# Float64 weights unpacked into adjacent words, from paged DRAM

## The chip, the cores and the metric

The kernel runs on one core of a Trainium2 chip. The metric is the device time of one execution in microseconds; the median of three runs is given beside the profiled execution.

## The reference, cut to what matters

Three stages, each on 2304 tokens of width 512 (4 batches of 576 tokens, 8 heads of 64):

```
attention   softmax(q k^T / 8 within a causal window of 64) v, per head, float32
dense       xn = x / sqrt(mean(x^2) + 1e-6) * rms_g
            g = xn @ w_gate;  val = xn @ w_val;  out = (g * sigmoid(g) * val) @ w_out     d_ff = 1536
top-2       8 experts 512 -> 1024 -> 512, two per token by noisy logits, weighted sum
```

`w_gate`, `w_val` (512 x 1536) and `w_out` (1536 x 512) are float64; everything else is float32. [...]

## The kernel before, in words

The dense stage is cut into 6 blocks of 384 tokens (j) and 12 chunks of 128 hidden units (fc); a step s = 12 j + fc does one chunk for one block. A step is two halves of products (`m1_half`, gate and value, 12 matmuls of 128 x 384 each, because activations and weights are each split into a high and a low part), tanh and products on the vector engines, and the output products (`m1_out`). Attention for the next block is laid between the steps.

The float64 weights are converted once, while block 0 runs, and stay in SBUF as float32: `gv[fc]` holds 512 columns of gate and 512 of value, `wo[fc]` 512 columns of the output weights, two chunks to a page. For every chunk there are three float64 tiles (c = 0, 1, 2), each 128 partitions x 512 numbers, that is 1024 32-bit words.

- `load_w` (lines 334 to 344) brings a tile into a raw page by one DMA on SP's queue. For gate and value, a partition gets four runs of 128 numbers (1 KB each); for `w_out`, one run of 4 KB.
- `conv_a` (346 to 350) is two ScalarE instructions: the high words, read as float32 and scaled, written back in place, every second word (line 349); the low words, read as unsigned integers and scaled into place as integers, also in place (350).
- `conv_b` (352 to 365) clamps the high words in place (line 361; on VectorE, or from chunk 2 on GpSimd for c = 0 and 2), shifts them left by 3 and ors in the low words (363, VectorE, written over the low words), and takes the sign from the high words into the float32 destination (364, VectorE).
- `split_w` and `split_o` (369 to 386) make the high and low parts of a chunk for each step: a ScalarE copy (372, 383) and a subtraction on VectorE or GpSimd (375, 384).

All of this draws on one pool of 24 pages of 4 KB per partition (tag "pg", line 68): the raw tiles, gv (12), wo (6), and the split parts of a step (three pages a step). A page is free again when the last instruction on its tile is done.

The written order is a table of slots, three to a step: chunk fc is loaded two slots before its first `conv_a`, `conv_a(fc, c)` stands in slot i + c and `conv_b(fc, c)` in slot i + c + 1 (lines 802 to 808), where i is the first slot of step fc - 2. A planner in the compiler takes this order as priorities and decides, from its own costs, where each instruction goes in its engine's queue; each engine then works its queue in order.

Of the kernel before, what the change touches and what calls it, by code (L numbers as in the profile page):

```python
# [7 lines left out]
F32 = mybir.dt.float32  # L8
F32R = mybir.dt.float32r
BF = mybir.dt.bfloat16  # L10
I32 = mybir.dt.int32
U32 = mybir.dt.uint32
AF = mybir.ActivationFunctionType
ALU = mybir.AluOpType
# [5 lines left out]
F64_HI = 122879.9921875 * 2.0 ** -112  # L20
# [3 lines left out]
def tile_window_attention_swiglu_top2(  # L24
# [16 lines left out]
    nc = tc.nc  # L41
    P = 128
# [1 line left out]
    N, E = noise.shape  # L44
    DM = H * D
    KD = DM // P
    FF = w_gate.shape[1]
    NF = FF // P
    F2 = w1.shape[2]
    NF2 = F2 // P  # L50
    HP = H // 2
# [18 lines left out]
    def page(dt, name):  # L70
        return pages.tile([P, 1024], dt, name=name, tag="pg", bufs=NPG)
# [30 lines left out]
    for h in range(2):  # L102
        s = slice(h * 64, h * 64 + 64)
        lo = float(-64 * h)
# [32 lines left out]
    CLP = (0, 2)  # L137
# [192 lines left out]
    gv, wo = {}, {}  # L330

    RAW = {}

    def load_w(fc, cs=(0, 1, 2)):
        fs = slice(fc * P, fc * P + P)
        srcs = (w_gate[:, fs].rearrange("(k p) f -> p k f", p=P), w_val[:, fs].rearrange("(k p) f -> p k f", p=P),
                w_out[fs, :])
        for c in cs:
            t = page(I32, f"raw{fc}_{c}")
            if c < 2:  # L340
                nc.sync.dma_start(t.rearrange("p (k f) -> p k f", k=KD), srcs[c].bitcast(I32))
            else:
                nc.sync.dma_start(t, srcs[c].bitcast(I32))
            RAW[fc, c] = t.rearrange("p (n w) -> p n w", w=2)

    def conv_a(fc, c):
        raw = RAW[fc, c]
        hi, lo = raw[:, :, 1].bitcast(F32), raw[:, :, 0]
        nc.scalar.activation(hi, hi, AF.Copy, scale=2.0 ** -112)
        nc.scalar.activation(lo, lo.bitcast(U32), AF.Copy, scale=0.936 * 2.0 ** -29)  # L350

    def conv_b(fc, c):
        raw = RAW.pop((fc, c))
        if c == 0:
            gv[fc] = page(F32, f"gv{fc}")
        if c == 2 and fc % 2 == 0:
            t = page(F32, f"wo{fc}")
            wo[fc], wo[fc + 1] = t[:, :512], t[:, 512:]
        dst = wo[fc] if c == 2 else gv[fc][:, c * 512:c * 512 + 512]
        hi, lo = raw[:, :, 1], raw[:, :, 0]  # L360
        (nc.gpsimd if c in CLP and fc > 1 else nc.vector).tensor_scalar(
            hi.bitcast(F32), hi.bitcast(F32), F64_HI, -F64_HI, op0=ALU.min, op1=ALU.max)
        nc.vector.scalar_tensor_tensor(lo, hi, 3, lo, op0=ALU.logical_shift_left, op1=ALU.bitwise_or)
        nc.vector.scalar_tensor_tensor(dst.bitcast(I32), hi, -0x80000000, lo, op0=ALU.bitwise_and,
                                       op1=ALU.bitwise_or)

    WS = {}

    def split_w(s):
        fc = s % NF  # L370
        h, l = page(F32R, f"gvH{s}"), page(F32R, f"gvL{s}")
        nc.scalar.activation(h, gv[fc], AF.Copy)  # L372
        for c, eng in enumerate((nc.vector, nc.gpsimd if s in GH else nc.vector) if s < NF else (nc.vector,)):
            f = slice(512 * c, 512 * c + 512) if s < NF else slice(0, 1024)
            eng.tensor_tensor(l[:, f], gv[fc][:, f], h[:, f].bitcast(F32), op=ALU.subtract)  # L375
        WS[s] = [h, l]
        if s > 0:
            split_o(s)

    def split_o(s):  # L380
        fc = s % NF
        o = page(F32R, f"woHL{s}")
        nc.scalar.activation(o[:, :512], wo[fc], AF.Copy)  # L383
        nc.gpsimd.tensor_tensor(o[:, 512:], wo[fc], o[:, :512].bitcast(F32),  # L384
                                                           op=ALU.subtract)
        WS[s].append(o)
# [3 lines left out]
    def m1_half(s, part):  # L390
        j = s // NF
        h, l = WS[s][:2]
        ps = bank(f"gv{s}_{part}", [P, TB])
        n = 0
        for kk in range(KD):
            c = slice(part * 512 + kk * P, part * 512 + kk * P + P)
            for a, b in ((h[:, c], xnH[j][:, kk, :]), (h[:, c], xnL[j][:, kk, :]), (l[:, c], xnH[j][:, kk, :])):
                nc.tensor.matmul(ps, a, b, start=n == 0, stop=n == 3 * KD - 1)  # L398
                n += 1
        PG[s, part] = ps  # L400
# [21 lines left out]
    def m1_out(s):  # L422
        j, fc = divmod(s, NF)
        hh = HT.pop(s)
        o = WS.pop(s)[2]
        if fc == 0:
            X2[j] = [psum.tile([P, 512], F32, name=f"x2_{j}_{t}", tag=f"x2_{t}", bufs=1) for t in range(TT)]
        for t in range(TT):
            c = slice(t * P, t * P + P)
            for n, (a, b) in enumerate(((hh[:, 0, c], o[:, :512]), (hh[:, 0, c], o[:, 512:]), (hh[:, 1, c], o[:, :512]))):  # L430
                nc.tensor.matmul(X2[j][t], a, b, start=fc == 0 and n == 0, stop=fc == NF - 1 and n == 2)  # L431
# [350 lines left out]
    for c in range(3):  # L782
        at(WL[c], load_w, 0, (c,))
    at(WL[3], load_w, 1)
    at(CS[0], conv_a, 0, 0)
    at(CS[1], conv_b, 0, 0)
    at(CS[2], conv_a, 0, 1)
    at(CS[3], conv_b, 0, 1)
    at(CS[4], split_w, 0)
    at(13, norm_a, 0)  # L790
    at(14, norm_b, 0)
    at(15, norm_c, 0)
    at(16, after_norm, conv_a, 0, 2)
    at(16, after_norm, conv_b, 0, 2)
    at(16, after_norm, split_o, 0)
    for c in range(3):
        at(17, after_norm, conv_a, 1, c)
        at(17, after_norm, conv_b, 1, c)
    at(WL[4], load_w, 2)
    for i in range(18):  # L800
        run(i)
# [36 lines left out]
    for s in range(NB * NF):  # L838
        j, fc = divmod(s, NF)
# [101 lines left out]
    for c in sorted(set(CAPS)):  # L941
        for e in range(E):
            if CAPS[e] == c and (e == 0 or CAPS[e - 1] != c):
                n = next((i for i in range(e, E) if CAPS[i] != c), E)
# [203 lines left out]
```

## Time and profile before

| | us |
|---|---|
| median of 3 runs (lowest, highest) | 1116.79 (1116.41, 1118.46) |
| profiled execution | 1118.05 |
| its span, first to last instruction | 1116.3 |
| PE busy | 1055.7 (95%) |
| VectorE (DVE) busy | 614.8 (55%) |
| ScalarE (ACT) busy | 555.1 (50%) |
| GpSimd (POOL) busy | 439.9 (39%) |
| DMA packets | 116408, of which 82048 under 512 B and 94576 under 2 KB |

The busy shares are averages over stages with different limits. In a row, PE is the matrix engine and PEld its weight loads, DVE is VectorE, ACT ScalarE, POOL GpSimd, and SPq the queue of SyncE, which issues DMAs; a number such as L364 is the line of the kernel. The arrow in a name such as gv<-raw goes from the tile read to the tile written.

### The profile page before, as it was taken

What the parts mean: (1) busy time and instruction counts of PE and PEld (TensorE: products, weight loads), DVE (VectorE), ACT (ScalarE), POOL (GpSimd) and SP (SyncE); (2) the same over time, 40 slices, a digit from 0 to 9 for tenths busy, and PEclk for the clock granted to TensorE, in tenths of its full rate; (3) what the DMA queues carried; (4) which work ended last, traced back from release to release, by engine and by line L of the source; (5) the groups of instructions that cost most, each with busy time, mean ns of one, the idle gap of its engine ahead of it and who ended that gap; (6) DMA issues with size and microseconds to landing.
All of it is one profiled execution on the core that took longest, in us unless ns stands there. A gap on an engine that the chain in (4) does not pass through costs nothing. (4 is left out here: it accounts for less than half of the span.)

```text
span 1116.3 us, 17685 instructions
## 1 busy us (share of the span) xinstructions
PE 1055.7 (95%) x6452; PEld 940.9 (84%) x6452; DVE 614.8 (55%) x1620; ACT 555.1 (50%) x1265; POOL 439.9 (39%) x456
## 2 busy tenths in 40 slices
PE   7688889999999999999999999899999999999993
PEld 6577778989899998989989888798989898989882
DVE  4899995666565575656666743342425253434330
ACT  6767766656555665655552513333334343433420
POOL 4366662352154225214422336333434354444311
PEclk9799999999999999999999999899999999999997
DMA  7846527111120211100021407435445444455312
GB/s 176 243 138 206 147 67 256 35 44 43 30 55 12 70 32 43 44 15 2 1 67 24 147 12 191 108 108 100 142 96 147 95 140 95 140 99 152 79 15 27
DMA packets 116408, 101.64 MB, mean 91 GB/s; under 512 B 82048, under 2 KB 94576, under 8 KB 116320
## 3 DMA queue, kind: packets, MB, share of 16 engines
q0 software_dynamic: 17904, 49.07, 18.5%
q1 hardware_dynamic: 98416, 51.42, 16.5%
q8 instruction: 52, 0.85, 0.3%
q14 instruction: 36, 0.29, 0.1%
HBM read 80.55 MB, written 19.92 MB: 90 GB/s over the span
## 5 line engine op out<-in xcount | busy, mean ns | idle before, releaser
L398 PE MATMUL gv<-xnH,gvH 128*128 128x384 f32 x576 | 204.2, 356 | 4.1 <-ACT xnH L325 3.2
L889 PE MATMUL y<-wH,hh 128*128 128x512 f32 (+1 forms) x608 | 203.4, 401 | 0.0
L398 PE MATMUL gv<-xnH,gvL 128*128 128x384 f32 x576 | 196.3, 343 | 4.5 <-DVE gvL L375 4.5
L398 PE MATMUL gv<-xnL,gvH 128*128 128x384 f32 x576 | 196.2, 341 | 0.0
L431 PE MATMUL x<-woHL,hh 128*128 128x512 f32 x648 | 174.1, 403 | 4.9 <-ACT hh L416 4.1
L384 POOL TENSOR_TENSOR woHL<-wo,woHL 128x512 fp32r<-128x512 f32 x72 | 99.3, 1380 | 146.5 <-ACT woHL L383 146.3
L431 PEld LDWEIGHTS x<-woHL,hh 128*128 128x128 f32 x648 | 118.8, 189 | 27.9 <-ACT hh L416 4.9
L889 PEld LDWEIGHTS y<-wH,hh 128*128 128x128 f32 (+1 forms) x608 | 113.8, 187 | 29.6 <-issue 0.2
L910 POOL DMA_INDIRECT out_dram<-ys,tid x38 | 62.2, 1636 | 190.7 <-ACT ys L903 145.2
L600 DVE TENSOR_TENSOR wL<-st,wH 128x1024 fp32r<-128x1024 f32 x64 | 78.3, 1226 | 100.9 <-ACT wH L599 98.3
L713 PE MATMUL h<-xph,wL 128*128 128x272 f32 (+3 forms) x448 | 133.3, 298 | 0.1
L713 PE MATMUL h<-xpl,wH 128*128 128x272 f32 (+3 forms) x448 | 133.4, 298 | 0.0
L713 PE MATMUL h<-xph,wH 128*128 128x272 f32 (+3 forms) x448 | 133.3, 298 | 0.0
L723 DVE SCALAR_TENSOR_TENSOR hh<-h,hh 128x272 fp32r<-128x272 f32 (+6 forms) x232 | 69.8, 325 | 111.1 <-ACT hh L719 91.8
L889 PE MATMUL y<-wL,hh 128*128 128x512 f32 (+2 forms) x328 | 129.1, 397 | 0.0
L719 ACT ACTIVATE hh<-h 128x160 fp32r<-128x160 f32 (+4 forms) x184 | 61.5, 343 | 128.6 <-PE h L713 86.8
L398 PEld LDWEIGHTS gv<-xnH,gvH 128*128 128x128 f32 x576 | 109.6, 191 | 7.7 <-ACT xnH L325 4.0
L398 PEld LDWEIGHTS gv<-xnH,gvL 128*128 128x128 f32 x576 | 109.2, 190 | 6.3 <-DVE gvL L375 5.9
L398 PEld LDWEIGHTS gv<-xnL,gvH 128*128 128x128 f32 x576 | 109.6, 190 | 0.8
L375 DVE TENSOR_TENSOR gvL<-gv,gvH 128x1024 fp32r<-128x1024 f32 (+1 forms) x73 | 90.8, 1245 | 15.0 <-ACT gvH L372 12.3
L245 POOL TENSOR_TENSOR pm<-pm,st 128x384 f32<-128x384 f32 x48 | 41.1, 857 | 134.5 <-DVE st L244 101.0
L372 ACT ACTIVATE gvH<-gv 128x1024 fp32r<-128x1024 f32 x72 | 75.6, 1050 | 22.7 <-PE gv L398 15.2
(208 smaller groups left out, 1925.9 us busy)
## 6 DMA issues: line engine op xcount, KB each, us to landing
vw<-in_v_dram SPq DMA_DIRECT2D x60, 128.0 KB
raw<-in_moe_w_gate_dram SPq DMA_DIRECT2D x12, 512.0 KB
raw<-in_moe_w_val_dram SPq DMA_DIRECT2D x12, 512.0 KB
raw<-in_moe_w_out_dram SPq DMA_DIRECT2D x12, 512.0 KB
out_dram<-zero SPq DMA_DIRECT2D x1, 4864.0 KB
qs<-in_q_dram SPq DMA_DIRECT2D x48, 96.0 KB
ks<-in_k_dram SPq DMA_DIRECT2D x48, 96.0 KB
x2d<-xs SPq DMA_DIRECT2D x18, 256.0 KB
```

The lines of the kernel that those rows point to most:

```text
L245: nc.gpsimd.tensor_tensor(p, p, st[:, :, 3:4].to_broadcast([P, 3, P]), op=ALU.mult)
L372: nc.scalar.activation(h, gv[fc], AF.Copy)
L375: eng.tensor_tensor(l[:, f], gv[fc][:, f], h[:, f].bitcast(F32), op=ALU.subtract)
L384: nc.gpsimd.tensor_tensor(o[:, 512:], wo[fc], o[:, :512].bitcast(F32), op=ALU.subtract)
L398: nc.tensor.matmul(ps, a, b, start=n == 0, stop=n == 3 * KD - 1)
L431: nc.tensor.matmul(X2[j][t], a, b, start=fc == 0 and n == 0, stop=fc == NF - 1 and n == 2)
L600: nc.vector.tensor_tensor(lo, a, ho.bitcast(F32), op=ALU.subtract)
L713: nc.tensor.matmul(ps, w, x, start=i == 0, stop=i == 3 * KD - 1)
L719: nc.scalar.activation(hh[:, c0 - p0:c1 - p0], ps[:, c0 - lo:c1 - lo], AF.Relu)
L723: nc.vector.scalar_tensor_tensor(hh[:, l.start + a - s.start:l.start + b - s.start], ps[:, a + p0 - lo:b + p0 - lo], 0.0, hh[:, a:b].bitca ...
L889: nc.tensor.matmul(ps[:a.shape[1]], a, b, start=i == 0, stop=i == len(terms) - 1)
L910: nc.gpsimd.indirect_dma_start(out=out, out_offset=bass.IndirectOffsetOnAxis(ap=r[:m], axis=0), in_=y[:m], in_offset=None, compute_op=ALU. ...
```

## The change

The three float64 weights lie in DRAM as pages of 128 x 512 numbers, one for each chunk, so that every load is 4 KB of adjacent bytes per partition. ScalarE writes the high words to their float32 destination (`target`: half of a gv page, or half of a wo page) as adjacent words, and the low words as adjacent words into the first half of the raw page. VectorE or GpSimd clamps in the destination; the shift writes the low words in the raw page; the sign step writes the destination in place. The destination's page is taken in `conv_a` instead of `conv_b`. The number of instructions on each engine stays the same.

```diff
--- before.py
+++ after.py
@@ -44,8 +44,7 @@
     N, E = noise.shape
     DM = H * D
     KD = DM // P
-    FF = w_gate.shape[1]
-    NF = FF // P
+    NF = w_gate.shape[0]
     F2 = w1.shape[2]
     NF2 = F2 // P
     HP = H // 2
@@ -332,37 +331,35 @@
     RAW = {}
 
     def load_w(fc, cs=(0, 1, 2)):
-        fs = slice(fc * P, fc * P + P)
-        srcs = (w_gate[:, fs].rearrange("(k p) f -> p k f", p=P), w_val[:, fs].rearrange("(k p) f -> p k f", p=P),
-                w_out[fs, :])
         for c in cs:
             t = page(I32, f"raw{fc}_{c}")
-            if c < 2:
-                nc.sync.dma_start(t.rearrange("p (k f) -> p k f", k=KD), srcs[c].bitcast(I32))
-            else:
-                nc.sync.dma_start(t, srcs[c].bitcast(I32))
-            RAW[fc, c] = t.rearrange("p (n w) -> p n w", w=2)
+            nc.sync.dma_start(t, (w_gate, w_val, w_out)[c][fc].bitcast(I32))
+            RAW[fc, c] = t
+
+    def target(fc, c):
+        if c < 2:
+            if fc not in gv:
+                gv[fc] = page(F32, f"gv{fc}")
+            return gv[fc][:, c * 512:c * 512 + 512]
+        if fc not in wo:
+            t = page(F32, f"wo{fc}")
+            wo[fc], wo[fc ^ 1] = t[:, :512], t[:, 512:]
+        return wo[fc]
+
 
     def conv_a(fc, c):
         raw = RAW[fc, c]
-        hi, lo = raw[:, :, 1].bitcast(F32), raw[:, :, 0]
-        nc.scalar.activation(hi, hi, AF.Copy, scale=2.0 ** -112)
-        nc.scalar.activation(lo, lo.bitcast(U32), AF.Copy, scale=0.936 * 2.0 ** -29)
+        words = raw.rearrange("p (n w) -> p n w", w=2)
+        nc.scalar.activation(target(fc, c), words[:, :, 1].bitcast(F32), AF.Copy, scale=2.0 ** -112)
+        nc.scalar.activation(raw[:, :512], words[:, :, 0].bitcast(U32), AF.Copy, scale=0.936 * 2.0 ** -29)
 
     def conv_b(fc, c):
-        raw = RAW.pop((fc, c))
-        if c == 0:
-            gv[fc] = page(F32, f"gv{fc}")
-        if c == 2 and fc % 2 == 0:
-            t = page(F32, f"wo{fc}")
-            wo[fc], wo[fc + 1] = t[:, :512], t[:, 512:]
-        dst = wo[fc] if c == 2 else gv[fc][:, c * 512:c * 512 + 512]
-        hi, lo = raw[:, :, 1], raw[:, :, 0]
-        (nc.gpsimd if c in CLP and fc > 1 else nc.vector).tensor_scalar(
-            hi.bitcast(F32), hi.bitcast(F32), F64_HI, -F64_HI, op0=ALU.min, op1=ALU.max)
+        lo = RAW.pop((fc, c))[:, :512]
+        hi = target(fc, c)
+        (nc.gpsimd if c in CLP and fc > 1 else nc.vector).tensor_scalar(hi, hi, F64_HI, -F64_HI, op0=ALU.min, op1=ALU.max)
+        hi = hi.bitcast(I32)
         nc.vector.scalar_tensor_tensor(lo, hi, 3, lo, op0=ALU.logical_shift_left, op1=ALU.bitwise_or)
-        nc.vector.scalar_tensor_tensor(dst.bitcast(I32), hi, -0x80000000, lo, op0=ALU.bitwise_and,
-                                       op1=ALU.bitwise_or)
+        nc.vector.scalar_tensor_tensor(hi, hi, -0x80000000, lo, op0=ALU.bitwise_and, op1=ALU.bitwise_or)
 
     WS = {}
 
@@ -1135,6 +1132,9 @@
     for name in _INS:
         a = _np.ascontiguousarray(inputs[name])
         if a.dtype == _np.float64:
+            if name != "moe_w_out":
+                a = a.reshape(4, 128, -1, 128).transpose(2, 1, 0, 3)
+            a = _np.ascontiguousarray(a.reshape(-1, 128, 512))
             a = a.view(_np.int64)
         arrays[f"in_{name}_dram"] = a
         args.append(nc.dram_tensor(f"in_{name}_dram", a.shape, _mybir.dt.from_np(a.dtype), kind="ExternalInput").ap())
```

## Rows read from the trace of the kernel before

**Rows 1.** Windows: stage, length, busy PE, PEld, DVE, ACT, POOL; clock, DMA share, GB/s.
```profile
28.00:60.00 32.00, 20.99 (x115) 18.34 (x113) 26.56 (x56) 21.47 (x49) 12.02 (x12) 0.74 0.88 249
60.00:90.00 30.00, 26.43 (x164) 22.94 (x162) 28.47 (x55) 22.16 (x53) 19.88 (x19) 0.99 0.50 158
90.00:120.00 30.00, 26.52 (x187) 22.54 (x187) 28.59 (x58) 24.98 (x62) 20.99 (x18) 1.00 0.57 175
120.00:158.00 38.00, 31.37 (x174) 26.82 (x173) 35.04 (x52) 24.65 (x53) 27.62 (x24) 0.96 0.41 115
158.00:1090.00 932.00, 921.10 (x5614) 827.13 (x5614) 482.46 (x1312) 440.24 (x977) 341.97 (x319) 1.00 0.31 79
```
**Rows 2.** Waits, 28 to 160 us: who waited for whom, total us, times, longest.
```profile
ACT woHL L383 <- DVE wo L364: 6.1, 5, 3.4
PEld gv L398 <- DVE gvL L375: 5.9, 4, 3.4
PEld x L431 <- ACT hh L416: 4.9, 2, 3.2
PE gv L398 <- ACT xnH L325: 3.2, 2, 1.9
DVE raw L361 <- ACT raw L349: 2.1, 3, 0.9
```
**Rows 3.** Lines: a line's engine, operation, shape, count | busy us, mean ns | idle before.
```profile
L363 DVE SCALAR_TENSOR_TENSOR raw<-raw 128x512 int32<-128x512 int32 x36 | 38.2, 1076 | 1.1 <-POOL raw L361 0.5
L350 ACT ACTIVATE raw<-raw 128x512 int32<-128x512 uint32 x36 | 24.3, 674 | 0.0
L349 ACT ACTIVATE raw<-raw 128x512 f32<-128x512 f32 x36 | 24.3, 674 | 0.1
L361 POOL TENSOR_SCALAR raw<-raw 128x512 f32<-128x512 f32 x20 | 21.0, 1051 | 2.6 <-DVE hh L417 1.3 <-ACT raw L349 1.1
L364 DVE SCALAR_TENSOR_TENSOR gv<-raw 128x512 int32<-128x512 int32 x24 | 20.2, 862 | 0.2
L364 DVE SCALAR_TENSOR_TENSOR wo<-raw 128x512 int32<-128x512 int32 x12 | 12.0, 1003 | 0.1
L361 DVE TENSOR_SCALAR raw<-raw 128x512 f32<-128x512 f32 x16 | 11.1, 694 | 2.2 <-ACT raw L349 2.1
```
**Rows 4.** One line's instructions: duration ns min/median/max, first and last start us.
```profile
L349 ACT ACTIVATE raw<-raw x36: 651/670/705, 28.1 to 148.7; 128x512 f32<-128x512 f32 x36
L361 POOL TENSOR_SCALAR raw<-raw x20: 701/1094/1117, 51.1 to 150.5; 128x512 f32<-128x512 f32 x20
L361 DVE TENSOR_SCALAR raw<-raw x16: 409/429/1611, 28.8 to 148.3; 128x512 f32<-128x512 f32 x16
L363 DVE SCALAR_TENSOR_TENSOR raw<-raw x36: 678/1104/1804, 29.3 to 155.1; 128x512 int32<-128x512 int32 x36
L364 DVE SCALAR_TENSOR_TENSOR gv<-raw x24: 676/681/1771, 30.5 to 152.6; 128x512 int32<-128x512 int32 x24
L364 DVE SCALAR_TENSOR_TENSOR wo<-raw x12: 676/1042/1481, 44.4 to 156.9; 128x512 int32<-128x512 int32 x12
L364 DVEq EVENT_SEMAPHORE  x1: 21/21/21, 151.1 to 151.1; - x1
```
**Rows 5.** Timelines of VectorE and GpSimd: start us, us, instruction.
```profile
28.85 1.05 POOL L245 TENSOR_TENSOR pm<-pm,st 128x384 f32<-128x384 f32 x1 [0.41 <-ACT raw L349]
29.34 1.11 DVE L363 SCALAR_TENSOR_TENSOR raw<-raw 128x512 int32<-128x512 int32 x1
81.75 0.69 DVE L364 SCALAR_TENSOR_TENSOR wo<-raw 128x512 int32<-128x512 int32 x1
82.26 0.70 POOL L361 TENSOR_SCALAR raw<-raw 128x512 f32<-128x512 f32 x1 [1.09 <-ACT raw L349]
```
**Rows 6.** Steps on adjacent words, from the lines, single lines and the timeline.
```profile
L375 DVE TENSOR_TENSOR gvL<-gv,gvH x13: 686/939/1816, 35.6 to 154.5; 128x512 fp32r<-128x512 f32 x13
160.32 1.21 DVE L375 TENSOR_TENSOR gvL<-gv,gvH 128x1024 fp32r<-128x1024 f32 x1
L414 DVE SCALAR_TENSOR_TENSOR th<-th,gv x11: 540/547/555, 58.5 to 153.9; 128x384 f32<-128x384 f32 x11
L213 DVE TENSOR_SCALAR qz<-pt 64x192 f32<-64x192 f32 x8 | 2.7, 342 | 0.0
L745 DVE MEMSET zero<- 128x512 f32 x1 | 0.5, 485 | 0.1
L190 POOL COPY vw<-vw x2: 605/608/611, 6.1 to 10.4; 64x512 f32<-64x512 f32 x2
L184 POOL MEMSET vw<- x2: 310/310/310, 28.1 to 34.3; 64x256 f32 x2
L218 POOL MEMSET kT<- x4: 142/152/153, 51.0 to 85.5; 128x64 f32 x4
L383 ACT ACTIVATE woHL<-wo x11: 612/627/653, 47.0 to 147.1; 128x512 fp32r<-128x512 f32 x11
```
**Rows 7.** Weight loads on SP's queue: issue ns, and SP's waits (us, times, longest).
```profile
L341 SPq DMA_DIRECT2D raw<-in_moe_w_gate_dram x12: 367/437/924, 21.0 to 138.3; - x12
L341 SPq DMA_DIRECT2D raw<-in_moe_w_val_dram x12: 368/452/719, 21.5 to 142.4; - x12
L343 SPq DMA_DIRECT2D raw<-in_moe_w_out_dram x12: 346/454/844, 29.6 to 142.8; - x12
SPq L341 <- DVE st L244: 9.1, 2, 8.9
SPq L341 <- DVE gv L364: 7.1, 2, 4.7
SPq L341 <- PE gv L398: 5.0, 2, 4.8
```
**Rows 8.** Timelines of ScalarE and VectorE around the last chunk's conversion.
```profile
145.01 0.67 ACT L349 ACTIVATE raw<-raw 128x512 f32<-128x512 f32 x1
145.58 0.68 ACT L350 ACTIVATE raw<-raw 128x512 int32<-128x512 uint32 x1
149.26 2.85 DVE L363 SCALAR_TENSOR_TENSOR raw<-raw 128x512 int32<-128x512 int32 x2
152.03 1.28 DVE L364 SCALAR_TENSOR_TENSOR gv<-raw 128x512 int32<-128x512 int32 x2
153.40 1.06 ACT L372 ACTIVATE gvH<-gv 128x1024 fp32r<-128x1024 f32 x1 [1.09 <-DVE rs L304]
```

## The prediction

> **What bounds the kernel now.** I read the windows first, to split the span into stages [rows 1]. From 158 to 1090 us the columns say PE 921.10 of 932: matrix work sets the pace there, and nothing in the change touches that stage (the last float64 chunk is converted before 158). All the edited lines run between 28 and 158 us. There PE leaves 11.0 us idle from 28 to 60 and 13.7 us from 60 to 158 (98 less 26.43, 26.52 and 31.37). In the same 60 to 158 VectorE is busy 92.1 of 98, ScalarE 71.8 and GpSimd 68.5. So VectorE bounds the block in which the weights are converted, and PE bounds what follows; a microsecond won or lost before 158 goes to the end nearly whole. How much there is to win at most is PE's idle time, 24.7 us, much of which (28 to 60) belongs to attention and the first norm.
>
> Next the waits of that stretch [rows 2]. PE waits for gvL (VectorE's subtract) 5.9 and for hh from ScalarE 4.9. ScalarE waits for wo (the last conversion step) 6.1, and the clamp waits for ScalarE's high word 2.1. No row of that answer names a DMA as what a compute engine waited for: the raw pages are there when ScalarE wants them.
>
> Then the lines of the conversion, one row per engine and output [rows 3]. VectorE: 38.2 for the shift, 20.2 and 12.0 for the sign, 11.1 for 16 clamps, 81.5 of its 118.7 us in this stretch. ScalarE: 24.3 for each of its two lines. GpSimd: 21.0 for 20 clamps. The medians and minima [rows 4] tell that much of it is not work: the shift has a minimum of 678 and a median of 1104 ns, the sign 676 and 681 (gv), 676 and 1042 (wo). What the excess is stands in one place of the timeline [rows 5]: a shift that starts at 29.34, when GpSimd's multiply runs from 28.85 to 29.90, takes 1.11 us, that is 0.55 behind the end of the multiply. 72 shift and sign steps at 0.68 would be 49.0 us; they take 70.4, so 21.4 us are standing behind GpSimd.
>
> **The change, part by part.**
>
> VectorE's shift and sign, 72 instructions: their operands move from every second word to adjacent words. What an adjacent-word step of the same size costs is shown by the split of 512 columns, two SBUF operands, minimum 686 ns [rows 6]; the split of 1024 takes 1.21 us, so 512 columns more cost 0.52, 1.02 ns each; the 384-column step of one SBUF and one PSUM operand is 547 at the median, and 128 columns more give 678. Against 676 to 678 for the spaced ones I take 0. Bounds: 10 ns dearer each (686 against 676), 0.7 us in all; cheaper, down to a 384-column step (0.54), 72 x 0.14 = 10 us, an end to which I give no weight, since the spaced 512 lies on the line of the contiguous ones.
>
> I weigh a rule here. The row first: spaced words cost VectorE nothing [rows 4, 6]. The Trainium skill (SBUF — State Buffer, Specifications (TRN2), and the note on cachelines under Door 1) says that SBUF is read in 16-byte lines and that a stride is free as long as two accesses fall in each line, so for 4-byte words two apart nothing is lost. By that rule the compaction is worth 0 on every engine and the time stays; VectorE's rows agree with it, ScalarE's next do not quite.
>
> VectorE's 16 clamps: minimum 409, median 429 ns for 512 columns. That is less than the contiguous write of 512 fp32 by a memset, 485 [rows 6], so the spaced clamp already goes faster than a column per step; I take 0. Bounds: dearer by 0.08 each, up to the memset, 1.2 us; cheaper by 0.07 each, down to the 192-column scaling of q (342, from PSUM), 1.1 us.
>
> GpSimd's 20 clamps: minimum 701 ns, median 1094. The shortest starts at 82.26 while VectorE's sign step of 81.75 + 0.69 is still running until 82.44 [rows 5], so its own work is about 0.52. Contiguous neighbours: a 64 x 512 copy, 608; memsets of 256 and 64 columns, 310 and 152, which drawn on give 0.52 for 512. I take 0; bounds 0 to 0.09 each (701 less 608), 1.8 us of GpSimd. VectorE stands behind GpSimd a third to a half of GpSimd's time, so at most 0.9 us of it reaches the path.
>
> ScalarE's 72 instructions: 0.67 us at the median spaced in and out; with adjacent words the split of 512 columns takes 0.627 [rows 4, 6]. In the new kernel they still read spaced words and only write adjacent ones. If the writes carry the 45 ns: 72 x 0.045 = 3.2 us; if the reads do: 0. I take half, 1.6 us. ScalarE is busy 71.8 of 98, so most of that falls into its idle time; where it leads (clamp behind the high word, 2.1 us of waits; xnH behind eight conversions at 40 to 45 us, where PE waits 3.2 for xnH [rows 2]) some third counts: 0.5 us. A cost against it: the low word is now written over words that the first instruction reads. Unsynchronised neighbours on ScalarE start 0.56 apart at a duration of 0.67 [rows 8]; if the second had to wait for the end of the first, it is 0.11 each, 36 x 0.11 = 4.0 us of ScalarE, a third of it 1.3 us on the path. I take 0.
>
> Weight loads: 24 of the 36 loads go from 512 runs of 1 KB to 128 of 4 KB, 12288 packets to 3072, and the page's 116408 to about 107190. The issue on SP costs the same for either form: 437 and 452 ns at the median for the two that change, 454 for w_out, which has 4 KB rows already [rows 7]. As no engine waits for raw, I take 0. The cover is ScalarE's queue of older work; were it gone, the high-word step would start at the landing. The loads themselves mostly wait for a free page (SP's rows: 7.1 for the sign step, 5.0 for PE, 9.1 behind an older wait [rows 7]), and a faster transfer does not free pages.
>
> Pages: the gv page of a chunk, and the wo page of two, are now taken by ScalarE's first step instead of VectorE's last. In the written order that is one of three slots earlier, and ahead of the three pages of the next split. There are 24 pages. When chunk 11 is converted, gv 0 to 10 hold 11, wo 6, raw 3, the split of the current step 3, the woHL of the step before 1: all 24. So gv 11 has to wait for a release, and now ScalarE stands there with everything behind it in its queue (tanh, hh, splits). I cost it at 0 in the forecast, since the planner places instructions with the release in view and can put other ScalarE work first, and I make it a rival.
>
> Sum: -0.5 (ScalarE), rounded up by a little from GpSimd, -0.6 us. The profiled execution took 1118.05 (span 1116.3 and 1.75 around it) and would become 1117.45; the median of the runs is 1116.79, 1.26 lower, so 1116.2.
>
> **The rivals.**
> Larger gain. All of ScalarE's 45 ns count on the path (3.2 us) and GpSimd's clamp gains 0.09 (0.9 of it on the path): -4.1 and, with one of the two partly hidden, -3.5: 1113.3. For it: the stretch is a chain through three engines (ScalarE, GpSimd or VectorE, ScalarE, VectorE, PE), so lead time counts too. Against: ScalarE idles a quarter of the stretch.
>
> Slower, the page wait. Place: chunk 11, with 10 and 9 in its wake. ScalarE's high-word step of (11,0) starts at 145.01, VectorE's first write into that gv page at 152.03, and only there does a sign step show a semaphore event of its own, at 151.1 [rows 4, 8]. If that is the page's release, the high word starts 6 us later: four ScalarE steps of 0.56 from 151.1 end at 153.4, clamp, shift and sign of the second half (0.43, 0.68, 0.68) at 155.3, against 153.3 before; the split at 153.40 follows it directly, and PE's first product of that chunk soon after. So 2.0 us, and half that again for the two chunks before: +3, 1119.8. It decides from a release later than about 149 (ScalarE has 4 us to spare there, since VectorE reaches the shift only at 149.26). For: 24 of 24 pages by my count, loads that wait for releases. Against: the release may be older, and other work can go first.
>
> Nothing. ScalarE's 45 ns belong to its reads, which stay spaced, the loads are hidden, and the planner's order holds: 1116.8. For it: every row of VectorE. Against: ScalarE's spaced rows. The line rule above would have it come out so.
>
> **How the numbers follow.** This kernel's runs tell a change of 0.2%, 2.2 us. Forecast (small gain) 0.36, its own range 1114.2 to 1118.0, since another order of the planner moves a wait of PE such as the longest for gvL, 3.4 us, either way; a quarter of it is beyond 2.2. Larger gain 0.27, slower 0.27, nothing 0.10. Faster: 0.27 + 0.09 = 0.36; slower 0.27 + 0.01 = 0.28; within: 0.36. The range reaches to the far sides of both rivals, where bounds add up (ScalarE 3.2 with 1.1 of VectorE's clamps; page wait 3 with 0.7 and some of 1.3): 1111.8 to 1121.0.
>
> **What would show it.** VectorE's shift and sign keep minima near 680 ns, its clamp near 410; ScalarE's two lines fall to 0.62 or stay at 0.67; the GpSimd clamp's mean stays near 1.05; packets fall to 107190. VectorE's busy time in 28 to 158 stays at 118.7 within 2. A ScalarE wait for PE, POOL or VectorE ahead of the high-word step, near 145 to 152, is the page wait. I am wrong if the shift and sign fall clearly below 0.65 us, if PE's idle time before 158 changes by more than 2 us, or if the time moves after 158.

## The result, and the profile after

The changed kernel takes 1134.04 us (median of 4 runs, 1131.0 to 1135.13) against 1116.86 us for the kernel before on the same chip: ratio 1.0142, 95% interval 1.0124 to 1.0161. That is 17 us slower, where 1116.2 us and a range up to 1121.0 were predicted. The profiled execution has a span of 1133.3 us.

The windows come first, in the columns of [rows 1] (PE, PEld, DVE, ACT, POOL busy; clock, DMA share, GB/s), of the kernel after:

```profile
28.00:60.00 32.00, 21.14 (x126) 19.12 (x126) 26.35 (x55) 20.94 (x48) 12.12 (x13) 0.84 0.80 234
60.00:90.00 30.00, 21.24 (x120) 18.66 (x119) 28.01 (x50) 23.56 (x52) 18.23 (x18) 0.89 0.50 159
90.00:120.00 30.00, 25.84 (x174) 22.38 (x174) 29.04 (x54) 21.04 (x53) 19.10 (x17) 1.00 0.59 166
120.00:158.00 38.00, 28.56 (x169) 24.76 (x168) 21.95 (x49) 24.35 (x57) 17.61 (x19) 0.91 0.43 132
158.00:200.00 42.00, 38.92 (x216) 35.57 (x215) 30.75 (x61) 22.82 (x52) 15.93 (x14) 0.92 0.37 133
200.00:1107.00 907.00, 894.17 (x5446) 801.97 (x5446) 463.12 (x1264) 422.04 (x933) 330.94 (x311) 1.00 0.30 75
```

From 200 us on PE is busy 894.17 of 907 (98.6%), as it was before from 158 to 1090 (98.8% [rows 1]): the later stage is untouched, and the loss lies ahead of 200. VectorE, which bounded the conversion at 35.04 of 38 us in the window 120 to 158 [rows 1], is busy only 21.95 there: it stands waiting for work. The stretch from 28 to 200 us, of the kernel before and of the kernel after:

```profile
28.00:200.00 172.00, 147.31 (x898) 129.12 (x896) 147.46 (x291) 120.64 (x283) 91.90 (x83) 0.94 0.58 173
28.00:200.00 172.00, 135.70 (x800) 120.50 (x800) 136.10 (x266) 112.71 (x256) 82.99 (x79) 0.91 0.52 162
```

The trace holds 800 matmuls there, before 898. From 200 us on one takes 907 / 5446 = 0.1665 us, so the 98 that are missing are 16.3 us, about the whole loss. (The kernel with the DRAM pages alone, below, has 923 at the time of the kernel before, so this is good to some 4 us.) Not all of it is idle time: PE stands idle 36.3 us, before 24.7, which is 11.6 more, and by an estimate from the same two lines PE is busy 0.170 us for each matmul instead of 0.164, some 4.5 us for 800 (the shapes are mixed). The granted clock goes with that: 0.89 from 60 to 90 us and 0.91 from 120 to 158, before 0.99 and 0.96. From 136 to 139 us it is 0.50 of full speed, the lower of its two levels, after PE was busy for 0.22 of the 3 us before.

The place of the loss shows in ScalarE's tanh, one for each step; the start times come from the timelines of both kernels:

| tanh of step | 0 | 1 | 2 | 4 | 6 | 8 | 10 | 11 | 13 |
|---|---|---|---|---|---|---|---|---|---|
| before, us | 53.23 | 59.56 | 69.31 | 90.24 | 110.07 | 134.04 | 151.81 | 161.14 | 171.66 |
| after, us | 47.84 | 65.36 | 72.38 | 97.63 | 119.55 | 141.57 | 163.66 | 174.21 | 187.01 |
| later by | -5.4 | 5.8 | 3.1 | 7.4 | 9.5 | 7.5 | 11.9 | 13.1 | 15.4 |

The loss does not come at one chunk: step 0 is early, 5.8 us are lost by step 1, 9.5 by step 6 and 15.4 by step 13. Next the waits of SP's queue (total us, times, longest) from 28 to 180 us of the kernel after; L336 is the weight load:

```profile
SPq L336 <- DVE gv L362: 22.2, 6, 7.2
...
SPq L336 <- PE gv L395: 16.2, 3, 9.4
...
SPq L336 <- DVE wo L362: 10.1, 2, 7.0
```

Those releasers are the last users of a page. All of the weight loads' waits for an engine in that stretch (SP's rows for the load lines, added up) come to 50.3 us, before to 28.3; the rows in [rows 7] are the larger ones of those. Two stretches of ScalarE's timeline (start us, us, instruction; in brackets the idle time ahead of it) show the order of its work:

```profile
47.84 0.47 ACT L404 ACTIVATE th<-gv 128x384 f32<-128x384 f32 x1
...
54.76 0.66 ACT L353 ACTIVATE gv<-raw 128x512 f32<-128x512 f32 x1
59.39 0.33 ACT L214 ACTIVATE qz<-pt 64x192 f32<-64x192 f32 x1 [3.97 <-DVE qz L212]
...
61.28 0.69 ACT L354 ACTIVATE raw<-raw 128x512 int32<-128x512 uint32 x1
61.85 0.69 ACT L353 ACTIVATE gv<-raw 128x512 f32<-128x512 f32 x1
62.41 0.69 ACT L353 ACTIVATE wo<-raw 128x512 f32<-128x512 f32 x1
62.97 1.25 ACT L354 ACTIVATE raw<-raw 128x512 int32<-128x512 uint32 x2
64.82 0.63 ACT L380 ACTIVATE woHL<-wo 128x512 fp32r<-128x512 f32 x1 [0.60 <-DVE wo L362]
65.36 0.47 ACT L404 ACTIVATE th<-gv 128x384 f32<-128x384 f32 x1
...
147.14 0.52 ACT L413 ACTIVATE hh<-th 128x384 fp32r<-128x384 f32 x1 [2.56 <-DVE th L411]
147.57 0.47 ACT L253 ACTIVATE pT<-pp 128x384 f32<-128x384 f32 x1
149.28 0.49 ACT L404 ACTIVATE th<-gv 128x384 f32<-128x384 f32 x1 [1.23 <-PE gv L395]
151.19 0.33 ACT L271 ACTIVATE xT<-pv 128x192 f32<-128x192 f32 x1 [1.42 <-PE pv L267]
...
153.37 1.23 ACT L353 ACTIVATE wo<-raw 128x512 f32<-128x512 f32 x2 [1.18 <-PE gv L395]
154.50 1.20 ACT L353 ACTIVATE gv<-raw 128x512 f32<-128x512 f32 x2
```

At 61 to 64 us five conversion steps stand ahead of the tanh of step 1. Before, no conversion step stands right ahead of that tanh, which waits for PE:

```profile
59.56 0.49 ACT L407 ACTIVATE th<-gv 128x384 f32<-128x384 f32 x1 [0.93 <-PE gv L398]
```

At 153.37 the high-word steps of wo 10, wo 11 and gv 11 start together, once PE has let go of a page; before, the high-word steps had ended by 149.4 (the last starts at 148.7 [rows 4]) and only the sign step needed the page, at 151.1, where its semaphore event of 21 ns shows no wait. That is the page wait of the prediction's slower rival, at the place that it named. It is also the only wait of ScalarE's conversion steps for a page that the waits of this kernel show from 28 to 165 us (total us, times, longest):

```profile
ACT wo L353 <- PE gv L395: 1.2, 1, 1.2
```

The instructions themselves, in the columns of [rows 4], of the kernel after:

```profile
L353 ACT ACTIVATE gv<-raw x24: 646/660/687, 28.0 to 155.1; 128x512 f32<-128x512 f32 x24
L353 ACT ACTIVATE wo<-raw x12: 650/668/694, 39.3 to 153.9; 128x512 f32<-128x512 f32 x12
...
L354 ACT ACTIVATE raw<-raw x36: 647/666/717, 29.9 to 159.2; 128x512 int32<-128x512 uint32 x36
...
L359 DVE TENSOR_SCALAR gv<-gv x14: 411/427/1604, 28.7 to 155.8; 128x512 f32<-128x512 f32 x14
L359 POOL TENSOR_SCALAR gv<-gv x10: 611/614/1054, 49.7 to 155.3; 128x512 f32<-128x512 f32 x10
L359 POOL TENSOR_SCALAR wo<-wo x10: 614/750/1053, 58.5 to 154.7; 128x512 f32<-128x512 f32 x10
...
L361 DVE SCALAR_TENSOR_TENSOR raw<-gv,raw x24: 657/679/1779, 30.7 to 161.7; 128x512 int32<-128x512 int32 x24
...
L362 DVE SCALAR_TENSOR_TENSOR gv<-gv,raw x24: 670/686/1777, 31.9 to 164.8; 128x512 int32<-128x512 int32 x24
```

Only GpSimd's clamp became clearly faster, 611 against 701 ns at the minimum. Those two minima are not alike, though: the clamp of 701 ns is the one that starts at 82.26, beside VectorE's sign step [rows 5]. In two kernels with spaced words (the kernel before with 22 and with 23 pages, below) one clamp each, in that order, has no wide VectorE step beside it:

```profile
146.06 0.68 POOL L361 TENSOR_SCALAR raw<-raw 128x512 f32<-128x512 f32 x1 [0.68 <-ACT raw L349]
144.96 0.64 POOL L361 TENSOR_SCALAR raw<-raw 128x512 f32<-128x512 f32 x1 [2.67 <-ACT raw L349]
```

So the adjacent words are worth some 0.03 to 0.07 us to a clamp. VectorE's minima moved by 21 ns at most (shift 678 to 657, sign 676 to 670), ScalarE's medians by 2 to 10 ns (the high-word step from 670 to 660 and 668, the low-word step from 672 to 666). DMA packets fell from 116408 to 107192.

### The profile page after: what moved, and what is told of

It is laid out like the page before. It is cut to its first block, busy times and chain, and to the rows that moved or that the text cites. A ratio compares the mean times of both kernels' runs of the same rounds, so it can differ in the third digit from the quotient of the medians.

```text
span 1133.3 us, 17672 instructions
## 1 busy us (share of the span) xinstructions
PE 1059.8 (94%) x6452; PEld 946.6 (84%) x6452; DVE 612.9 (54%) x1620; ACT 556.7 (49%) x1265; POOL 431.3 (38%) x456
## 2 busy tenths in 40 slices
DMA packets 107192, 101.64 MB, mean 90 GB/s; under 512 B 82048, under 2 KB 82288, under 8 KB 107104
## 5 line engine op out<-in xcount | busy, mean ns | idle before, releaser
L395 PE MATMUL gv<-xnH,gvH 128*128 128x384 f32 x576 | 206.6, 359 | 6.2 <-ACT gvH L369 4.9
L907 POOL DMA_INDIRECT out_dram<-ys,tid x38 | 59.5, 1566 | 194.9 <-ACT ys L900 151.5
L372 DVE TENSOR_TENSOR gvL<-gv,gvH 128x1024 fp32r<-128x1024 f32 (+1 forms) x73 | 89.3, 1224 | 11.8 <-ACT gvH L369 9.7
L710 PEld LDWEIGHTS h<-xpl,wH 128*128 128x128 f32 x448 | 84.3, 188 | 1.8 <-issue 1.5
```

The costliest lines, as they stand in the source:

```text
L710: nc.tensor.matmul(ps, w, x, start=i == 0, stop=i == 3 * KD - 1)
L907: nc.gpsimd.indirect_dma_start(out=out, out_offset=bass.IndirectOffsetOnAxis(ap=r[:m], axis=0), in_=y[:m], in_offset=None, compute_op=ALU. ...
```

## The experiments

The theory (P in the expectations): ScalarE's first step takes the float32 page while the raw page is still held, so each tile under conversion occupies more of the 24 pages for longer; weight loads and conversions then wait for pages, and the steps behind them come late. Its rivals in turn: the DRAM pages, the wait of the low-word step for the high-word step, the planner's order alone, ScalarE standing at the page wait. (The letter W stands for the wait of the low-word step in the first expectations, and for the wo page as the blocker in later ones.) All ratios are to the kernel before, run on the same chip.

### DRAM pages alone

The kernel before with the new DRAM layout and nothing else:

```diff
-                nc.sync.dma_start(t.rearrange("p (k f) -> p k f", k=KD), srcs[c].bitcast(I32))
...
+            nc.sync.dma_start(t, (w_gate, w_val, w_out)[c][fc].bitcast(I32))
```

> The kernel before with the weights as contiguous DRAM pages and nothing else; words stay spaced in the raw page. Theory P (the float32 page is taken one slot earlier, so that loads and ScalarE wait for free pages): no effect of the loads, 1117 within 2 us. Rival D (loads that land earlier or differently make the planner order the block worse): about 1134. Rival W (adjacent words themselves, the low word written over words that the high-word step reads, make the order worse): 1117.

Measured: 1118.87 us, ratio 1.000 (0.9989 to 1.0012). The DRAM layout neither gains nor costs.

### Low words in place

The changed kernel, but the low words stay where they are, every second word, so that ScalarE's second step overwrites nothing that its first one reads:

```diff
-        nc.scalar.activation(raw[:, :512], words[:, :, 0].bitcast(U32), AF.Copy, ...
+        nc.scalar.activation(words[:, :, 0], words[:, :, 0].bitcast(U32), AF.Copy, ...
...
-        lo = RAW.pop((fc, c))[:, :512]
+        lo = RAW.pop((fc, c)).rearrange("p (n w) -> p n w", w=2)[:, :, 0]
```

> The changed kernel, but the low words stay spaced in place (no write over words that the high-word step reads); the high words go to the gv or wo page early, DRAM pages as in the change. Theory P: 1130 to 1136. Rival W: back to 1115 to 1120. Rival D: about 1134.

Measured: 1131.66 us, ratio 1.0103 (1.0084 to 1.0122). Most of the loss stays; the edit is worth some 0.4%, which is no more than the scatter met below.

### Pages claimed early, words as before

The kernel before, with a one-column ScalarE copy into each gv and wo page ahead of the high-word step, 18 copies of 0.194 us:

```diff
+        if c == 0:
+            gv[fc] = page(F32, f"gv{fc}")
+            nc.scalar.activation(gv[fc][:, 0:1], hi[:, 0:1], AF.Copy)
...
+            nc.scalar.activation(t[:, 0:1], hi[:, 0:1], AF.Copy)
```

> The kernel before, words spaced and DRAM unchanged, but conv_a claims the gv page (c = 0) and the wo page (c = 2, even chunk) with a copy of one column on ScalarE: 18 added instructions of about 0.2 us. Theory P: most of the loss appears, 1128 to 1136, with longer waits of SP for pages from chunk 9 on. Rivals D and W: only the added instructions, 1117 to 1120.

Measured: 1122.92 us, ratio 1.004 (1.0025 to 1.0055). That is outside what either side expected, and far less than P did. The 18 copies are 3.5 us of ScalarE's time themselves, so how much of the 0.4% is the page is not shown. P as first put, that holding the page is all, falls. The high-word steps of c = 0 and of every other wo stand behind the page here too, since they overwrite the word that the copy reads; those of c = 1 and of the second half of a wo page are free of it. The lag in block 0 is partly there: the tanh of step 1 starts 4.7 us later than before (64.24) and that of step 6 7.4 later (117.50), against 5.8 and 9.5 in the changed kernel; but that of step 13 is only 3.7 late (175.38), against 15.4. What adds the rest at the last chunks is not shown by this run.

### Pages taken late

The changed kernel, but the high words go to three 2 KB buffers that are idle in block 0; the sign step writes gv or wo and takes the page there, as before the change:

```diff
+        HI[fc, c] = work.tile([P, DM], F32, name=f"hi{fc}_{c}", tag="xs", bufs=3)
-        nc.scalar.activation(target(fc, c), words[:, :, 1].bitcast(F32), AF.Copy, scale=2.0 ** -112)
+        nc.scalar.activation(HI[fc, c], words[:, :, 1].bitcast(F32), AF.Copy, scale=2.0 ** -112)
...
-        nc.vector.scalar_tensor_tensor(hi, hi, -0x80000000, lo, op0=ALU.bitwise_and, op1=ALU.bitwise_or)
+        nc.vector.scalar_tensor_tensor(dst, hi, -0x80000000, lo, op0=ALU.bitwise_and, op1=ALU.bitwise_or)
```

> The changed kernel, adjacent words and DRAM pages, but the high words go to three buffers of 2 KB that lie idle in block 0 (those of the block-end evacuation), and the float32 page is taken by the sign step again, as before the change. Theory P: the loss is gone, and as the changed kernel was 5.7 us ahead at the split of step 6, some of that is kept: 1111 to 1117. Rivals D and W: still about 1130 or more.

Measured: 1115.5 us, ratio 0.9977 (0.996 to 0.9994). The whole loss is gone, with the adjacent words, the wait of the low-word step and the DRAM pages all still there. (The kernel uses 6 KB more in block 0 than the one before, the three buffers, which may be part of the 0.2%.) SP's waits for pages (28 to 180 us), of this kernel:

```profile
SPq L336 <- DVE gv L367: 4.6, 3, 2.8
...
SPq L336 <- PE gv L400: 1.7, 1, 1.7
```

### Late for some: by chunk and by kind

The same edit under a condition, the others early: `fc > 6`, `fc < 7`, gv alone (`c < 2`), wo alone (`c == 2`):

```diff
...
+        hi = work.tile([P, DM], F32, name=f"hi{fc}_{c}", tag="xs", bufs=3) if fc > 6 else target(fc, c)
...
```

Late from chunk 7 on: 

> The changed kernel, but from chunk 7 on the high words go to three separate 2 KB buffers and the sign step takes the gv or wo page late; chunks 0 to 6 take it early as in the changed kernel. Theory P (the loss is the page taken early once the 24 pages are full, from chunk 7 on): as with late pages for all chunks, 1113 to 1119 us, and the ScalarE split of step 10 starts at 143 to 148. Rival S (what counts is the earlier placement of every chunk, the early ones too: their loads and splits are displaced before the pool is full): the loss stays for the most part, 1126 to 1134 us.

Late up to chunk 6: 

> The changed kernel with late pages for chunks 0 to 6 only, early pages from chunk 7 on. Theory P (full pool from chunk 7 on): the loss stays, 1127 to 1135 us, the ScalarE split of step 10 starts at 153 or later. Rival S (early placement of the first chunks): back to 1114 to 1120 us.

Late gv alone: 

> The changed kernel with late pages for gv (gate and value) alone; the wo page, one for two chunks, is still taken by ScalarE's first step. Theory P: gv takes a page for every chunk, wo for every second one, and both kinds were seen waiting to 153 us, so gv late gives back more than half: 1118 to 1124 us. Rival W (the wo page is the blocker, since it is taken first for the even chunk and its second half stays empty until the odd one): the loss stays, 1128 to 1134 us.

Late wo alone: 

> The changed kernel with the late page for wo alone; the gv page is taken by ScalarE's first step. Theory P: less than half is given back, 1124 to 1132 us. Rival W (the wo page is the blocker): back to 1115 to 1120 us.

Measured: 1123.45 us, ratio 1.0059 (1.0042 to 1.0076), late from chunk 7 on; 1123.16, 1.0048 (1.003 to 1.0066), up to chunk 6; 1109.25, 0.9936 (0.992 to 0.9953), gv alone; 1122.64, 1.0056 (1.0039 to 1.0073), wo alone. All four expectations missed on the time. Either half of the chunks gives back a good half of the loss, wo alone gives back 61% where P allowed less than half, and gv alone gives back more than all; these shares do not add up, so they do not divide the loss by chunk or by kind. That the pool fills only from chunk 7 on was wrong; SP's loads run ahead as far as pages go, and the first long wait of a weight load after the change is that for the load at 64.85 us, which stands 7.1 us behind the end of the one ahead of it (57.32 + 0.43; before, the same load stood 5.0 us behind, at 61.74). It is for chunk 5, so it cannot be what makes step 1 late at 65.36; there the trace shows only the order in ScalarE's queue. The tanh of step 1 starts at 65.04 us with early pages in the first chunks, at 56.88 with late ones (after: 65.36, before: 59.56). The early wo page does no harm once gv is late. The gv page costs with the three buffers in use on either side: from wo late (1.0056) to all late (0.9977), where only gv's place changes, it is 0.8%. The timeline of ScalarE from 46 to 64 us with gv late, where the first three tanh stand 8.3 and 8.6 us apart:

```profile
46.17 0.49 ACT L410 ACTIVATE th<-gv 128x384 f32<-128x384 f32 x1 [0.35 <-PE gv L401]
...
52.97 0.68 ACT L358 ACTIVATE raw<-raw 128x512 int32<-128x512 uint32 x1
54.47 0.49 ACT L410 ACTIVATE th<-gv 128x384 f32<-128x384 f32 x1 [0.82 <-PE gv L401]
54.86 0.66 ACT L357 ACTIVATE wo<-raw 128x512 f32<-128x512 f32 x1
...
62.51 0.64 ACT L357 ACTIVATE wo<-raw 128x512 f32<-128x512 f32 x1
63.05 0.47 ACT L410 ACTIVATE th<-gv 128x384 f32<-128x384 f32 x1
```

Late gv a second time: 

> The late gv page with the early wo page a second time: the ratio 0.9936 stands, 0.992 to 0.996 (about 1109 us); were it chance, 0.998 to 1.002.

Measured: 1110.44 us, ratio 0.9951 (0.9938 to 0.9965): it stands. This version beats both kernels.

Late gv and the low words in place: 

> The late gv page with the early wo page (1109.25 us by itself), and the low words left in place, so that ScalarE's second step writes nothing that its first one reads and need not wait for it. If that wait costs what the same edit gave in the changed kernel (0 to 4 us): 1105 to 1109 us. If the wait is hidden: 1108 to 1111. If the spaced low words cost the shift something, or the planner's order falls differently: up to 1116.

Measured: 1116.41 us, ratio 1.0002 (0.9991 to 1.0012), just past the last of the expected ranges. The same edit that took 0.4% off the changed kernel puts 0.6% on this one. The tanh of its step 5 starts 1.5 us behind that of late gv alone (94.00 and 92.54), that of step 10 5.9 behind (147.19 and 141.24). The edit takes a wait away and adds no work, so the likeliest cause left is the order that the planner makes of it; this is argued, not shown. If so, order alone can move this kernel by some 6 us, and the gain of late gv may be of that kind too.

### Fewer and more pages

The kernel before with 22 and with 23 pages (`NPG = 22`, `NPG = 23`).

22 pages: 

> The kernel before with 22 pages instead of 24. A page taken early is held some 4 to 8 us longer per chunk of about 9 us, which is about one page at a time for gv and half of one for wo. Theory P: two pages fewer does to the kernel before what the early pages did, 1124 to 1140 us. Rival O: the pool has slack in the kernel before, 1116 to 1121 us.

23 pages: 

> The kernel before with 23 pages instead of 24. 22 pages gave 1140 us, 24 us more. Theory P, even price of a page: 1124 to 1132 us. If the pool has one page of slack and then falls off: 1116 to 1119 us.

Measured: 1140.16 us, ratio 1.0219 (1.0189 to 1.0249), with 22; 1121.53, 1.0052 (1.0037 to 1.0068), with 23. Both lie outside what was expected of them (1140.16 by a hair). The first page costs 5 us, no more than the 6 us that order alone may move, the second 19: at the latest from the second page on, the pool has no slack in the kernel before. The weight loads' waits of the kernel with 22 pages, SP's queue, 28 to 180 us:

```profile
SPq L341 <- DVE gv L364: 14.3, 3, 5.9
SPq L341 <- PE gv L398: 10.7, 2, 6.7
SPq L341 <- DVE wo L364: 10.2, 3, 4.4
...
SPq L343 <- DVE gv L364: 4.6, 1, 4.6
```

Its weight loads wait for an engine 51.0 us in all, as those of the changed kernel do with 24 pages (50.3).

The changed kernel with 25 pages; three double buffers elsewhere are made single for room, and a control has these with 24 pages:

```diff
-    NPG = 24
+    NPG = 25
...
-            sq = work.tile([P, KD, P], F32, name=f"sq{j}_{t}", tag="sq", bufs=2)
+            sq = work.tile([P, KD, P], F32, name=f"sq{j}_{t}", tag="sq", bufs=1)
...
```

25 pages: 

> The changed kernel with a pool of 25 pages instead of 24; to make room, three double buffers outside the conversion (sq, xth, xtl) are single. Theory P (the page held earlier makes the pool too small): one page more gives back a third or more of the 17 us, 1118 to 1128 us, at least 4 us under the same kernel with 24 pages. Rival O (the loss is another order of the planner or a wait inside the conversion, not the number of pages): within 3 us of the same kernel with 24 pages.

The control: 

> The control to it: the changed kernel with the same three buffers single and 24 pages. Both theories: 1131 to 1137 us, as the changed kernel, if the three buffers are of no weight in block 0; they may cost up to 5 us at the norm and the router of each block, which the kernel with 25 pages then pays too.

Measured: 1148.38 us, ratio 1.0282 (1.0257 to 1.0306), and 1150.21, 1.0319 (1.0282 to 1.0356). The 25th page gives back 1.8 us by the medians, with intervals that overlap: not the 4 us or more of theory P, but within the 3 us of rival O. The weight loads' waits do not fall either, 49.8 us with 25 pages and 50.4 with 24. The single buffers alone cost some 17 us, though, which weakens the pair as a test. Something of the page is seen in block 0: the tanh of step 10 starts at 156.16 us with 25 pages, at 166.15 with 24; by step 13 the lead is down to 4.6 (186.13 against 190.68).

### Early page, raw page free early

The changed kernel with its early pages, but the low words go to the three idle buffers, so that the raw page is free right after ScalarE:

```diff
+        LO[fc, c] = work.tile([P, DM], I32, name=f"lo{fc}_{c}", tag="xs", bufs=3)
-        nc.scalar.activation(raw[:, :512], words[:, :, 0].bitcast(U32), AF.Copy, scale=0.936 * 2.0 ** -29)
+        nc.scalar.activation(LO[fc, c], words[:, :, 0].bitcast(U32), AF.Copy, scale=0.936 * 2.0 ** -29)
```

> The changed kernel with its early gv and wo pages, but the low words go to three separate 2 KB buffers, so that the raw page comes free right after ScalarE's two steps instead of after VectorE's sign step. Theory P (occupied pages): the page taken early is paid back by the raw page freed early; 1112 to 1120 us, SP's page waits for weight loads (28 to 180 us) fall from 48 to under 20. Rival Q (ScalarE standing at the page wait): ScalarE still waits for the page first, the loss stays for the most part, 1126 to 1134 us.

Measured: 1122.2 us, ratio 1.0055 (1.0039 to 1.007). Some 60% of the loss is gone by the ratios (1.0142 to 1.0055), though the page is taken as early as in the changed kernel. The time lies between the two expectations; the waits of the weight loads, 16.9 us, are under 20 as P expected. What the weight loads wait for is now ScalarE's low-word step, no longer VectorE's sign step; SP's queue, 28 to 180 us:

```profile
SPq L336 <- ACT lo L357: 13.8, 5, 5.3
...
SPq L336 <- PE gv L398: 1.1, 1, 1.1
```

The kernel has a new wait of its own, as the low-word step needs one of three buffers that the sign step frees. From the lines, 28 to 180 us (busy us, mean ns, idle before):

```profile
L357 ACT ACTIVATE lo<-raw 128x512 int32<-128x512 uint32 x36 | 23.7, 666 | 4.8 <-DVE gv L365 4.8
```

### The runs side by side

| kernel | ratio | waits of weight loads for an engine, 28 to 180 us | matmuls, 28 to 200 us |
|---|---|---|---|
| gv late | 0.9936 | 19.2 | 950 |
| gv late again | 0.9951 | 18.5 | 943 |
| all late | 0.9977 | 8.7 | 939 |
| before | 1 | 28.3 | 898 |
| DRAM pages alone | 1.000 | 27.9 | 923 |
| gv late, low words in place | 1.0002 | 11.8 | 912 |
| claimed early | 1.004 | 34.1 | 880 |
| late up to chunk 6 | 1.0048 | 32.7 | 876 |
| before, 23 pages | 1.0052 | 38.7 | 878 |
| low words apart | 1.0055 | 16.9 | 857 |
| wo late | 1.0056 | 45.6 | 864 |
| late from chunk 7 | 1.0059 | 45.0 | 859 |
| low words in place | 1.0103 | 44.3 | 801 |
| after | 1.0142 | 50.3 | 800 |
| before, 22 pages | 1.0219 | 51.0 | 873 |
| after, single buffers, 25 pages | 1.0282 | 49.8 | 802 |
| after, single buffers, 24 pages | 1.0319 | 50.4 | 762 |

The waits of the loads go with the time in the main, within some 6 us. Exceptions are the kernel of low words apart (its wait sits on ScalarE), gv late with the low words in place (11.8 us of waits at the time of the kernel before, which has 28.3), and the kernels with single buffers, whose loss has another source. That the two go together does not show which is the cause: a load also waits longer for a page when the work that frees it is late. With 22 pages much of the loss comes after 200 us: at 200 it is 25 matmuls behind, 4 us, which is no more than this count scatters.

## Why the prediction was wrong, point by point

**The step that failed** is "Pages ... I cost it at 0 in the forecast, since the planner places instructions with the release in view and can put other ScalarE work first". The runs put 17 us in its place: with the page late again, and the other parts of the change kept, the loss is gone (0.9977). It is the price of the early page in this kernel, not of an early page as such: claimed early in the kernel before, it costs 0.4% with its copies. Other ScalarE work does stand first, but not to the good: conversion steps stand ahead of the tanh at 61 to 64 us, and between 144 and 153 ScalarE stands idle for 6.4 us (2.56, 1.23, 1.42 and 1.18 in the timeline), of which only the last ends with the release of a page.

**The rival** had the sign and the part of the change that costs, and the wait near 145 to 152 us is there (153.37), but as 1.2 us of ScalarE's time. Its price, +3, was mis-sized. It counted pages at one moment, at chunk 11, and took the pool as slack before that; a weight load already waits 7.1 us from 57.75 us on, and early pages in the chunks up to 6 alone cost 0.6%. And it priced ScalarE standing at the page; what the runs show instead is weight loads that wait longer, 50.3 us against 28.3, and another order of ScalarE's work. The lower end of the prediction's whole range does not follow from its terms either: those named there, 3.2 and 1.1, taken from 1116.8 as the rivals are, give 1112.5 and not 1111.8.

**The signs of being wrong** that it named came: PE's idle time from 28 to 158 us went from 24.7 to 33.2 us, where 2 us were allowed, and PE is busy 3.1 us less from 158 to 200 (38.92 against 42.00). VectorE's busy time from 28 to 158 fell from 118.7 to 105.4 us.

**VectorE's shift and sign at 0, its clamp at 0**: right in size; the minima moved by 21 ns at most, the clamp's median from 429 to 427. The rule of the Trainium skill that was weighed there (SBUF — State Buffer, Specifications (TRN2), on 16-byte lines) agrees with these rows; GpSimd's clamp, 0.64 to 0.68 us spaced and 0.61 to 0.62 adjacent, does not quite follow it.

**GpSimd's clamp at 0, bounds to 0.09**: the gain, 0.03 to 0.07 us, lies inside the bounds. The step's 0.52 us, read from one start beside a VectorE step, was too low by some 0.1. Its mean did not stay near 1.05: it is 0.78 in the kernel after. That goes with what stands beside it, not with the words: with pages taken late and the words adjacent its median is 1051 ns again.

**ScalarE, half of 45 ns**: too much; 2 to 10 ns came. Its rows with spaced reads keep 0.66 us and more, whether they write adjacent words or not. The cost against it, the low-word step behind the high-word step, was taken as 0; taking it away gave 0.4% in one kernel and lost some 0.6% in the other, so it was not told from the scatter between edits.

**Weight loads at 0, packets to 107190**: right; ratio 1.000 with the pages alone, 107192 packets.

**The sum's own range**, 1114.2 to 1118.0, allowed the planner one wait of 3.4 us either way; late gv with the low words in place shows some 6 us, if that is the planner's order.

What is shown is which part of the change costs: the early page, gv's above all. What stays open is how: how the 17 us divide between loads that start late and the planner's order that puts conversion ahead of the tanh; no run held the order fixed while the page was taken early, and a 25th page did not shorten the waits. Why late gv gains 0.5% on the kernel before is open as well.

## What to carry to other kernels

A buffer from a shared pool is best taken by the last instruction that needs it, not by the first: moving it up the chain by two or three instructions went with a loss of 17 us here, where the whole change of words had been priced at 4 at best. Where loads prefetch into the same pool as the results, look at the waits of the load queue over the whole stretch, not at the pages of the busiest moment; dropping a page or two from the kernel before gives a scale for a page before the change is made (5 and 24 us here, the first within the scatter). And time a change of layout apart from the change of allocation that comes with it.

## What the runs showed of the hardware

GpSimd, unlike VectorE, pays a little for spaced words: with no wide VectorE step beside it, the clamp of 128 x 512 takes 0.64 to 0.68 us on every second word and 0.61 to 0.62 on adjacent ones; VectorE's takes 409 and 411 ns at the minimum. On ScalarE it seems to be the spaced read that costs: 0.66 to 0.67 us with spaced reads whichever way it writes, against 0.627 for the split of the same size on adjacent words [rows 6]. The split and the conversion differ in their output type too, so this is not a clean pair. TensorE's granted clock fell to 0.50 in the conversion stretch of the kernel after (136 to 139 us), behind 3 us in which PE was busy for 0.22; by the estimate from the windows above, slower matmuls add some 4.5 us to the 11.6 us that PE stands idle longer.
